# Attention with pooled keys and a squared-ReLU feed-forward: five blocks of chunk 0 in split form, eleven weight tiles used in place

## The chip, the cores and the metric

The kernel runs on one core of a Trainium2 chip. A core has five engines that run side by side, each with its own instruction queue, worked through in order: TensorE (PE: matrix products, and PEld for the loading of their weights), VectorE (DVE), ScalarE (ACT), GpSimd (POOL) and SyncE (SP, here a queue for DMAs only). They meet through semaphores. The metric is the device time of one execution, in microseconds.

## The reference

q, k and v have the shape (8 batches, 8 heads, 576 tokens, 64), all float32. Keys and values are averaged over 8 neighbouring tokens, so that 72 remain; attention goes over these, and the result feeds a network with 2048 hidden columns:

```python
k_p = k.reshape(B, H, Sp, pool, D).mean(axis=3)
v_p = v.reshape(B, H, Sp, pool, D).mean(axis=3)
scores = scale * np.matmul(q, k_p.transpose(0, 1, 3, 2))
scores = scores - np.max(scores, axis=-1, keepdims=True)
attn = np.exp(scores)
attn = attn / (np.sum(attn, axis=-1, keepdims=True) + 1e-09)
attn_out = np.matmul(attn, v_p)
...
x = np.ascontiguousarray(attn_out.transpose(0, 2, 1, 3)).reshape(B * S, H * D)
h = np.maximum(x @ w_in, 0.0)
return (h * h @ w_out).astype(np.float32)
```

x has 4608 rows and 512 columns. The weights arrive as eight-byte floats, taken as pairs of 32-bit words, and the kernel turns them into float32 itself.

## The kernel before

**Chunks, blocks and steps.** The 4608 rows are worked through in 9 chunks of 512 (`c`), the 2048 hidden columns in 16 blocks of 128 (`fc`). The main loop (lines 857 to 912) runs over 144 steps and three more, one step for each pair of chunk and block. In a step PE computes the first product of its block (`hidden`, tile h: x times w_in), then the attention work listed for that step (`on_pe`: scores, transposes of keys, the product with the values, av), then the second product of the block three steps back (`project`, tile o: the squared ReLU, r, times w_out; `LAG` is 3). Steps 0 to 15 are chunk 0, steps 16 to 31 chunk 1. The o of block 12 of chunk 0 is in step 15.

**Plain and split.** In chunk 0 both products take float32 operands as they are; the profile shows two records for each such matmul, 8 in a block's product. From chunk 1 on an operand is split into a rounded high part and the rest, both of type float32r, and three matmuls take the place of one: high times high, high times low, low times high (`three`, line 539), 12 in a block's product, in this order for each of four groups of 128 rows. The split of r makes gh (ACT copies) and gl (DVE subtracts); `split_hidden` (628) orders both two steps after the block's first product, gl through the list `behind`, which `catch_up` empties: in odd steps right after the second product, in even steps later. From chunk 2 on the first product is done with seven products in place of eight (`seven`), with sums that DVE and ACT make in PSUM (h, u).

**The weights.** A tile of w_out lands as raw words (`land`, SP queue), ACT takes two passes over it (`magnitude`), DVE three (`to_float32`: one TENSOR_SCALAR and two SCALAR_TENSOR_TENSOR). Several tiles of one step go through DVE together. The float32 tile wf_o serves chunk 0. Then `store_weights` (201) splits it into w_o (ACT copies, DVE subtracts), `send_weights` (206) writes w_o to DRAM (tile kept), and `fetch_weights` (211) brings it back for each later chunk, one step before its use. The steps of all this come from `need`: for tiles 11 to 15 of w_out the conversion is in steps 12, 13, 14, 15 and 16, `magnitude` one step before, `land` three before. `store_weights` of tile i is in step 10 + i, `send_weights` one later, and chunk 1 fetches tile i in step 18 + i.

**Buffers.** A pool of 40 slots in SBUF (`w_tile`) holds weights, raw tiles and operands. r has two buffers from chunk 1 on; in chunk 0 r uses the six of gh and gl. PSUM has eight banks: four for o, two for h, two of tag "a" for everything of the attention (keys kps, scores sps, turned exponents pps, av), which a tile holds until its last reader is through.

**Keys and scores.** `turn_k` (287) turns the pooled keys of a batch, pair of heads by pair, with a PE transpose into one bank (kps), and ACT copies them out (kf). For batch 1 this is `late_turn_k` (316) in step 3, at the end of the step, behind the second product. Pair 3 of these keys is the last that POOL sums up (kq). `token_scores` of chunk 1's pair 0 is in step 4 and takes both banks "a" (sps); DVE takes minima of them (tm), ACT eight exponents, four from each bank (te).

From chunk 2 on the stages of a pair of heads are `transpose_q` (DVE turns q into qs; ACT casts and DVE subtracts to get st), `scores` (PE; ACT copies sc out; POOL reduces it to the maximum, mx), `exponents` (DVE subtracts, ACT takes exponents, POOL reduces to the sum, tot), then the sums go through DRAM to a reciprocal that is broadcast (rs, rc, rr, rd, rb), and `weigh_values` (PE: av; DVE multiplies with rb into xf). `x_sums` and `x_operand` make of xf the operands x_B and x_T. `STEADY` and `EARLY` give the steps of the pairs, `START` holds back some of chunk 2.

**Order in a step.** `todo` holds what is due. Behind the second product and what follows from it come, in chunk 0, ReLU and square (`activate`), then loads, then the list in order of entry (`magnitude`, `send_weights`, `transpose_q`, `exponents`, ...), then `to_float32`, then the splits (`split_quarter` for w_in, `store_weights`); in chunk 1 `activate` follows behind these.

## Time and profile before

| | us |
|---|---|
| median of 3 runs | 910.28 (909.4 to 911.02) |
| profiled execution, time | 910.27 |
| profiled execution, span from first to last instruction | 908.5 |
| granted clock of PE, mean | 0.999 |
| PE / PEld / DVE / ACT / POOL busy | 894.3 / 715.2 / 568.1 / 509.6 / 421.1 |
| second product, plain (o<-wf_o,r), 128 records | 58.4 |
| second product, split (o<-w_o,gh and o<-w_o,gl), 1536 records | 322.3 + 200.9 |
| w_o<-kept, 128 transfers | 512 KB each |

The span is shared by PE's work and PE's gaps; all helpers record their instructions under one line (34), so the tables go by the names of tiles: `o<-w_o,gh` is the second product reading w_out's split tile and gh. In a timeline a row gives the start, the length, the engine, the operation, what it writes and reads, how many instructions are merged, and in square brackets the idle time before it with the engine and tile that ended it. Matmuls are pipelined, so a row's length overlaps the next one; the chain of waits gives the times from one to the next.

### The profile page before, as it was taken

To read this page: it belongs to the slowest core of one execution; us is meant where nothing else is said; L and a number is where in the kernel's file an instruction comes from. 1 tells how busy PE (TensorE), PEld (TensorE's weight loads), DVE (VectorE), ACT (ScalarE), POOL (GpSimd) and SP (SyncE) were. 2 spreads that over 40 slices of the span, in tenths; PEclk is the share of its full clock that TensorE was granted. 3 is DMA by queue.
4 is the path that set the end of the run, shared out by engine and by line. 5 is a ranking of instruction groups with operands and counts; after the bars stand their busy time and mean duration, and the time that the engine had idled before them with its cause. 6 is when DMAs were issued, how large, how long until landed. Compare 5 with 4: busy or idle time off the path is not lost.

```text
span 908.5 us, 14140 instructions
## 1 busy us (share of the span) xinstructions
PE 894.3 (98%) x5090; PEld 715.2 (79%) x5093; DVE 568.1 (63%) x946; ACT 509.6 (56%) x1017; POOL 421.1 (46%) x227
## 2 busy tenths in 40 slices
PE   8999999999999999999999999999999999999998
PEld 5444445777878888888888888888888888889987
DVE  7997778668688877456755575648544653353222
ACT  5866756656565656554655556455644564344442
POOL 3753245566555456566555655564444444200000
PEclk9999999999999999999999999999999999999999
DMA  9898574877555666665575556654533353245401
GB/s 222 263 261 189 140 177 110 229 227 196 130 155 141 143 143 142 178 156 118 133 207 135 120 143 179 153 132 117 170 109 113 105 164 116 96 173 197 175 1 47
DMA packets 157335, 138.72 MB, mean 153 GB/s; under 512 B 94488, under 2 KB 122136, under 8 KB 157264
## 3 DMA queue, kind: packets, MB, share of 16 engines
q1 hardware_dynamic: 128464, 127.13, 46.5%
q0 software_dynamic: 28800, 10.68, 10.3%
q8 instruction: 40, 0.66, 0.3%
q14 instruction: 31, 0.25, 0.1%
HBM read 119.65 MB, written 18.06 MB: 152 GB/s over the span
## 4 chain that ended last, share of the span: by engine, by line
PE 82%; DMA 6%; DVE 4%; ACT 2%; POOL 2%; issue 2%; SPq 1%; DVEq 0%; ACTq 0%; POOLq 0%
PE o L34 40%; PE h L34 35%; PE av L34 3%; PE sps L34 3%; SPq L34 1%; DMA rb<-rd 1%; POOL k L34 1%; DMA k<-in_k_dram 1%; DMA v<-in_v_dram 1%; DMA w_o<-kept 1%; DVE gl L34 1%; DVE wf_i L34 1%; DMA rd<-rr 1%; ACT sc L34 0%; DVE xf L34 0%
## 5 line engine op out<-in xcount | busy, mean ns | idle before, releaser
L34 PE MATMUL o<-w_o,gh 128*128 128x512 f32 x1024 | 322.3, 396 | 2.0 <-DMA w_o<-kept 2.0
L34 POOL PARTITION_ALL_REDUCE tot<-sc x56 | 187.8, 3403 | 86.4 <-issue 86.4
L34 PEld LDWEIGHTS o<-w_o,gh 128*128 128x128 f32 x1024 | 184.3, 188 | 46.8 <-issue 6.6
L34 PE MATMUL o<-w_o,gl 128*128 128x512 f32 x512 | 200.9, 392 | 0.0
L34 ACT ACTIVATE r<-h 128x512 f32<-128x512 f32 x144 | 83.6, 595 | 94.4 <-PE h L34 74.2
L34 PE MATMUL h<-x_T,w_S 128*128 128x256 f32 x1008 | 130.2, 283 | 0.5 <-ACT r L34 0.5
L34 POOL PARTITION_ALL_REDUCE mx<-sc x56 | 112.4, 2048 | 37.0 <-ACT sc L34 25.9
L34 PEld LDWEIGHTS h<-x_T,w_S 128*128 128x128 f32 x1008 | 124.9, 191 | 0.7 <-ACT r L34 0.7
L34 PEld LDWEIGHTS o<-w_o,gl 128*128 128x128 f32 x512 | 96.2, 188 | 21.3 <-DVE gl L34 0.4
L34 DVE TENSOR_TENSOR h<-h,u 128x256 f32<-128x256 f32 x168 | 72.6, 432 | 64.1 <-ACT u L34 33.7
L34 ACT COPY u<-h 128x256 f32<-128x256 f32 x112 | 41.8, 373 | 115.2 <-PE h L34 70.8
L34 PE MATMUL h<-x_B,w_A 128*128 128x256 f32 x672 | 98.6, 283 | 0.5 <-ACT r L34 0.5
L34 PEld LDWEIGHTS h<-x_B,w_A 128*128 128x128 f32 x672 | 91.6, 189 | 5.6 <-ACT r L34 1.1
L34 DVE TENSOR_TENSOR gl<-r,gh 128x512 fp32r<-128x512 f32 x128 | 92.1, 755 | 5.4 <-ACT gh L34 5.3
L34 POOL DMA_DIRECT2D k<-in_k_dram x36 | 44.1, 1225 | 109.1 <-issue 60.4
L34 POOL DMA_DIRECT2D v<-in_v_dram x36 | 44.1, 1224 | 107.4 <-issue 50.3
L34 DVE TENSOR_TENSOR u<-h,u 128x256 f32<-128x256 f32 x56 | 23.4, 417 | 101.9 <-ACT u L34 101.8
L34 ACT ACTIVATE r<-r 128x512 f32<-128x512 f32 x144 | 84.2, 625 | 1.1
L34 DVE TENSOR_TENSOR st<-qs,st 64x512 fp32r<-64x512 f32 x56 | 45.1, 806 | 61.8 <-ACT st L34 61.0
L34 ACT CAST gh<-r 128x512 fp32r<-128x512 f32 x128 | 78.9, 616 | 0.6 <-PE o L34 0.4
L34 ACT ACTIVATE sc<-sc 72x512 f32<-72x512 f32 x56 | 34.5, 632 | 69.3 <-DVE sc L34 69.3
L34 PE MATMUL h<-x,wf_i 128*128 128x512 f32 x128 | 57.8, 595 | 0.8 <-ACT x L34 0.8
(96 smaller groups left out, 1213.0 us busy)
## 6 DMA issues: line engine op xcount, KB each, us to landing
w_o<-kept SPq DMA_DIRECT2D x128, 512.0 KB
out_dram<-ob SPq DMA_DIRECT2D x36, 256.0 KB
raw_i<-in_moe_w_in_dram SPq DMA_DIRECT2D x16, 512.0 KB
raw_o<-in_moe_w_out_dram SPq DMA_DIRECT2D x16, 512.0 KB
kept<-w_o SPq DMA_DIRECT2D x16, 512.0 KB
rb<-rd SPq DMA_DIRECT2D x56, 128.0 KB
k<-in_k_dram POOLq DMA_DIRECT2D x36, 144.0 KB, 5.1
v<-in_v_dram POOLq DMA_DIRECT2D x36, 144.0 KB, 5.0
```

The costliest lines, as they stand in the source:

```text
L34: return lambda *a, **k: self.tc.keep_in_program_order(f(*a, **k))
```

## The change

Chunk 0's blocks from `WHOLE` = 11 on are treated as chunk 1's blocks are: r in its own two buffers, split into gh and gl, three matmuls in place of one. For that tiles 11 to 15 of w_out are converted in steps 12, 12, 13, 13 and 14, split in steps 12, 13, 13, 14 and 14 and written to DRAM in steps 13 to 17; chunk 1 fetches them as before. Tiles 0 to 10 are split in steps 16 to 26 instead of 10 to 20, written one step later, and chunk 1 reads the split tile where it is, without a fetch. Pair 3 of batch 1's keys is turned in step 4 instead of step 3, with a PSUM tile of its own. In chunk 1 `activate` comes ahead of the conversions and splits. For chunk 2, pair 0's `transpose_q` moves from step 9 to 8, pair 2's `transpose_q`, `scores` and `exponents` from 16, 18, 20 to 17, 19, 21; for chunk 3, pair 1's `exponents` and pair 2's `transpose_q` from step 32 to 33.

```diff
+    WHOLE = 11
...
-        stored[fc] = t
+        stored[fc] = wt["o", fc] = t
...
-    def late_turn_k(b):
-        turn_k(b)()
+    def late_turn_k(b, pairs=range(NPAIR)):
+        turn_k(b, pairs)()
...
-                if c == 0:
+                if c == 0 and f < WHOLE:
                     r = gts[c, f] = sb.tile([P, CH], F32, name=f"r_{c}_{f}", tag="gl" if f % 2 else "gh", bufs=3)
                 else:
                     r = gts[c, f] = sb.tile([P, CH], F32, name=f"r_{c}_{f}", tag="r", bufs=2)
...
     def split_hidden(c, fc):
-        if c == 0:
+        if c == 0 and fc < WHOLE:
             return
...
-            if c == 0:
+            if c == 0 and fc < WHOLE:
                 prods = [(g[:, tt], wf[key].rearrange("p a n -> p (a n)"))]
             else:
                 prods = [(g[x][:, tt], wt[key][:, w, :]) for x, w in three]
...
-    at(3, late_turn_k, 1)
+    at(3, late_turn_k, 1, range(NPAIR - 1))
+    at(4, late_turn_k, 1, [NPAIR - 1])
...
+    for i in range(WHOLE, NFC):
+        need["o", i] = WHOLE + 1 + (i - WHOLE) // 2
...
-        at(10 + i, store_weights, i)
-        at(11 + i, send_weights, i)
+        at(16 + i if i < WHOLE else (i + 14) // 2, store_weights, i)
+        at(17 + i if i < WHOLE else i + 2, send_weights, i)
...
-        for c in range(1, NCH):
+        for c in range(1 if i >= WHOLE else 2, NCH):
             at(c * NFC + i + LAG - STREAM, fetch_weights, c, i)
...
-    START = {transpose_q: 9, scores: 12, exponents: 13}
+    LATER = ((PLAIN + 1, 1, exponents), (PLAIN + 1, 2, transpose_q))
+    START = ({scores: 12, exponents: 13}, {}, {transpose_q: 17, scores: 19, exponents: 21}, {})
...
-                at(max(s + d, START[f]) if c == PLAIN and f in START else s + d - (f is transpose_q and (p != 2 if c >= PLAIN else p == 0)), f, c, p)
+                at(max(s + d, START[p].get(f, 0)) if c == PLAIN else s + d - (f is transpose_q and (p != 2 if c >= PLAIN else p == 0)) + ((c, p, f) in LATER), f, c, p)
...
+        if activate and s < PLAIN * NFC:
+            activate()
+            activate = None
```

## The prediction

> **What bounds the kernel now.** I read the page first, then PE's waits, then the chain that ended last, then each engine's timeline around the steps that the change touches. "Step s" is a turn of the main loop: the first product of block s, then the second product of block s − 3.

> ```profile
> PE 894.3 (98%) x5090; PEld 715.2 (79%) x5093; DVE 568.1 (63%) x946; ACT 509.6 (56%) x1017; POOL 421.1 (46%) x227
> DVE  7997778668688877456755575648544653353222
> ```

> PE is busy for 98% of the span. So a microsecond counts only if it is PE's own work or a gap of PE. DVE has room on average, but not in the first third (7 to 9 tenths), which is where the change puts more on it. The longest of PE's gaps, by what ended them:

> ```profile
> PE o L34 <- DMA w_o<-kept: 2.0, 2, 1.7
> PE sps L34 <- DVE xf L34: 1.5, 3, 0.9
> PE h L34 <- ACT r L34: 1.0, 2, 0.5
> ```

> With 0.8 us at kps (part 3) these 5.3 us hold every gap that the change can reach; beyond them only PE's own work can get less.

> **Part 1: five blocks of chunk 0 in split form.** From the chain of waits, with a plain second product (8 records), a split first product and a split second product (12 records):

> ```profile
> 143.92 3.43 PE o L34 x8
> 147.35 2.76 PE h L34 x12
> 150.12 3.43 PE o L34 x8
> ...
> 196.90 2.75 PE o L34 x12
> ```

> Plain costs 3.43 us a block, split 2.75, and next to each other they cost no more (143.92 to 150.12 is 3.43 + 2.76). Blocks 11 to 15: 5 × (3.43 − 2.75) = **−3.4 us**, PE's own work, so all of it on the path.

> **Part 2: the fetches of chunk 1.** Tiles 0 to 10 are now split at steps 16 to 26 and used in place, three steps later; 11 transfers of 512 KB are no longer issued.

> ```profile
> 191.16 0.71 PE L34 MATMUL o<-w_o,gh 128*128 128x512 f32 x2 [1.69 <-DMA w_o<-kept]
> 171.06 0.69 DVE L34 TENSOR_TENSOR w_o<-wf_o,w_o 128x512 fp32r<-128x512 f32 x1 [1.91 <-ACT w_o L34]
> 179.41 0.69 DVE L34 TENSOR_TENSOR gl<-r,gh 128x512 fp32r<-128x512 f32 x1 [0.38 <-ACT gh L34]
> ```

> The gap at 191.16 is step 22, tile 3. Its new split stands at step 19, where DVE does such a subtraction at 171, 20 us ahead, so **−1.7 us**. What is late next there is the gl of that block, and that is through at 180, 9 us before PE would ask for it. The 0.3 us that remain of the 2.0 belong to chunk 2 and stay. If the tile's place in DVE's order slipped by three steps, the gap would stay: 0 to −1.7.

> **Part 3: the last pair of batch 1's keys is turned one step later.** In step 3 PE waits for POOL's kq; in the new order pair 3 is turned at the end of step 4, behind the second product of block 1.

> ```profile
> 47.85 0.36 PE L34 MATMUL kps<-ident,kq 72*128 72x72 f32 x3
> 49.01 0.28 PE L34 MATMUL kps<-ident,kq 72*128 72x72 f32 x1 [0.80 <-POOL kq L34]
> 53.82 3.70 PE L34 MATMUL o<-wf_o,r 128*128 128x512 f32 x8
> 57.36 3.60 PE L34 MATMUL h<-x,wf_i 128*128 128x512 f32 x8
> ```

> The 0.8 goes. But the new kps needs a bank of tag "a", which has two, and in step 4 both hold the scores sps of chunk 1's pair 0. They come free when DVE has taken the minima and ACT the exponents:

> ```profile
> 58.07 0.81 DVE L34 TENSOR_REDUCE tm<-sps 128x4 f32<-128x288 f32 x2
> 58.60 1.80 ACT L34 ACTIVATE te<-sps,tm 128x72 f32<-128x72 f32 x8 [6.60 <-issue]
> ```

> The scores are through when PE's o starts, at 53.82, but DVE reaches the minima only at 58.07, and without a pause before them (the row has no idle time): it is still converting weights, and nothing ahead of them is changed. The first bank is free after four of eight exponents, 58.60 + 0.9 = 59.5, the second at 60.4. PE is there at 57.36 − 0.8 = 56.6, waits 2.9, turns the pair (about 0.25) and starts the next first product at 59.75 instead of 57.36: **+2.4 us** net. Behind the waiting kps stands all of PE. Bounds: −0.8 if no bank had to be waited for, +3.2 with the second bank. I take the first bank, the one that comes free first. PE's next gap is the one at 191.16, so this is not won back.

> **Part 4: DVE and ACT in steps 12 to 15.** Two tiles instead of one are converted in each of steps 12 and 13, and three more splits come ahead of the low half (gl) of block 12, which PE reads in step 15.

> ```profile
> 91.01 0.72 DVE L34 TENSOR_SCALAR wf_o<-wf_o 128x512 f32<-128x512 f32 x2
> 91.64 1.29 DVE L34 SCALAR_TENSOR_TENSOR wf_o<-wf_o,raw_o 128x512 uint32<-128x512 uint32 x2
> 92.85 1.28 DVE L34 SCALAR_TENSOR_TENSOR wf_o<-raw_o,wf_o 128x512 uint32<-128x512 uint32 x2
> ...
> 122.83 0.69 DVE L34 TENSOR_TENSOR x<-av,x 128x512 fp32r<-128x512 f32 x1 [3.30 <-ACT x L34]
> ...
> 132.47 3.77 DVE L34 SCALAR_TENSOR_TENSOR wf_o<-wf_o,raw_o 128x512 uint32<-128x512 uint32 x1
> 136.28 0.69 DVE L34 SCALAR_TENSOR_TENSOR wf_o<-raw_o,wf_o 128x512 uint32<-128x512 uint32 x1
> 136.88 2.73 DVE L34 TENSOR_TENSOR w_o<-wf_o,w_o 128x512 fp32r<-128x512 f32 x1
> 139.54 0.68 DVE L34 TENSOR_TENSOR w_A<-wf_i,w_A 128x512 fp32r<-128x512 f32 x1
> 140.14 1.25 DVE L34 TENSOR_TENSOR vp<-v 72x256 f32<-72x256 f32 x1
> 141.32 0.41 DVE L34 TENSOR_SCALAR wf_o<-wf_o 128x512 f32<-128x512 f32 x1
> 141.77 0.69 DVE L34 SCALAR_TENSOR_TENSOR wf_o<-wf_o,raw_o 128x512 uint32<-128x512 uint32 x1
> ```

> DVE's row of work starts when PE's av of step 12 is through (122.83, after a pause of 3.30), so it moves with PE and part 3 neither helps nor hurts it. gl of block 12 will come directly after the w_A whose successor starts at 140.14 now. New ahead of it: a pair of tiles (91.01 to 94.13, 3.1 us) for a single one (0.41 + 0.69 + 0.69 = 1.8), twice, +2.6; one more w_o and two gl at 0.6 each (139.54 to 140.14, start to start), +1.8. That gives 144.5.

> ```profile
> 123.87 0.66 ACT L34 ACTIVATE wf_o<-raw_o 128x512 f32<-128x512 f32 x1
> 124.42 0.67 ACT L34 ACTIVATE raw_o<-raw_o 128x512 uint32<-128x512 uint16 x1
> ```

> ACT has two more such passes over a raw tile (0.55 each from start to start) ahead of the casts of st, on which DVE then waits: half of their 1.1 reaches it, by my estimate, +0.6. POOL's next reduce, mx, now falls ahead of gl; beside it the vp at 140.14 took 1.25, of which I count 0.85 as lost, an estimate by the 0.41 that the next row needs for a tile of twice the size. Together about 146.0. PE reads gl as the third matmul of block 12: 143.92 − 0.68 (block 11 is shorter) + 0.46 = 143.7. So **+2.4 us**, rounded up by a semaphore's 0.1. Behind the waiting matmul stands all of PE; on ACT the r of block 13 waits for the gl of block 11 (two buffers r), behind it the exponents of chunk 2's pair 0 and POOL's sums, none of which PE reads before step 17. Afterwards steps 15 and 16 have no conversion any more (−1.8 each on DVE), and gl of block 13 comes out at about 151, when PE asks for it. Bounds: 0 if the sums move out of the way, and +5.9 from this:

> ```profile
> 133.04 7.02 POOL L34 PARTITION_ALL_REDUCE tot<-sc  x2
> 139.97 2.44 POOL L34 PARTITION_ALL_REDUCE mx<-sc  x1
> ```

> While POOL sums (7.02 us), three instructions of DVE of 0.69 take 3.77, 0.69 and 2.73: 5.1 us lost of the 7.02. Beside mx another of 0.69 (141.77) runs undisturbed. If each were held to the end of the reduces, DVE would lose 7.02 + 2.44 = 9.5 instead of 5.1 + 0.85 = 5.95, so 3.5 more, and PE would wait 5.9. [...]

> **Part 5: pair 2 of chunks 2 and 3 and pair 1's exponents a step later, relu and square ahead of the splits in chunk 1.** This touches two gaps at the start of chunk 2.

> ```profile
> 262.33 0.98 PE L34 MATMUL h<-x_B,w_A 128*128 128x256 f32 x6 [0.47 <-ACT r L34]
> 266.86 0.31 PE L34 MATMUL sps<-st,kl 128*72 128x192 f32 x1 [0.92 <-DVE xf L34]
> 270.15 0.88 PE L34 MATMUL h<-x_B,w_S 128*128 128x256 f32 x6
> 269.18 0.43 DVE L34 TENSOR_TENSOR h<-h,u 128x256 f32<-128x256 f32 x1 [0.44 <-ACT u L34]
> ```

> With the exponents and the transpose out of step 32, r and xf come sooner and both gaps (1.39) can close. But DVE's work from 253 to 270 is only reordered: its h at 269.6 is read by PE at 270.15, so only some 0.5 us can be won before this becomes the wait. **−0.5 us**; bounds −1.4 and +0.5 (st now stands closer to its scores, under POOL's sums).

> **Costed at nothing.** Five gl and gh of chunk 0 beyond block 12: DVE is ahead again. The raw tiles land up to two steps sooner: the SP queue has spare time there, since no store to DRAM waits in it before step 13. Pair 0's transpose for chunk 2 at step 8 instead of 9: a late q would hold DVE there, but the pause of 3.30 ahead of 122.83 takes up what DVE loses before it; without that pause it would be added to part 4.

> **Sum.** −3.4 − 1.7 + 2.4 + 2.4 − 0.5 = −0.8. The profiled execution took 910.27 (span 908.5 and 1.8 around it, which stays), the median is 910.28. Forecast: **909.5 us**, no change that counts; 0.2%, 1.8 us, is about what a measurement of this kernel can tell from none.

> **The rivals.**
> - DVE is in time for block 12 (its sums fall later, behind gl). For: ACT reaches the exponents about 3 us later than now. Against: even without ACT and mx gl comes at 144.5, unless less than the 5.1 us is lost ahead of it. Part 4 is 0: 907.1.
> - The turn of pair 3 meets a free bank. For: the old step 3 shows no wait for a bank. Against: two banks, two tiles of scores. Part 3 is −0.8: 906.3. With both, 903.9.
> - Slower: POOL's reduces hold DVE for their whole length in steps 13 and 14. Place: the third matmul of block 12; price 5.9 instead of 2.4; from 3.2 on the kernel is slower than before, from 5.0 on by more than 0.2%. 913.0. For: 3.77 and 2.73. Against: the 0.69 at 141.77.
> - The change doesn't do what it says: tile 3 is not ready in place and step 22 still waits. Against: 20 us of lead. 911.2.

> **How the numbers follow.** The forecast's case 0.55 (its own range 907.8 to 912.0 by the bank, part 5 and half a reduce more or less: 0.12 faster, 0.36 same, 0.07 slower); DVE in time 0.17; free bank 0.13; both 0.04; reduces that hold 0.08; no tile in place 0.03. Faster 0.46, same 0.39, slower 0.15. The range 905.5 to 912.3 leaves out the case of both, part of the reduces that hold and the ends of the rest.

> **What would show it.** Right: in PE's waits no w_o<-kept of 1.7; a kps that waits about 2.9 us for ACT te near 56.6; the o of block 12 waiting 2 to 3 us for DVE gl near 146; blocks 11 to 15 at 2.75 in the chain. Wrong: no wait at kps, no wait at gl, or PE gaps in chunk 1 at gl that the missing fetch had covered.

## The result and the profile after

| | before | after |
|---|---|---|
| median, 4 runs each | 910.19 (909.4 to 911.02) | 923.71 (920.92 to 924.89) |
| ratio, 95% interval | | 1.0144 (1.0119 to 1.0168) |
| profiled execution: time, span | 910.27, 908.5 | 923.6, 921.8 |
| PE busy | 894.3 | 897.7 |
| span less PE busy | 14.2 | 24.1 |
| granted clock of PE, mean | 0.999 | 0.994 |

The kernel is 13.3 us slower in span: 9.9 us of gaps, and 3.4 us more of PE's work, where the five split blocks should have made it 3.4 us less. First, PE's waits after the change, summed by what ended them (total, times, longest):

```profile
PE o L34 <- DVE gl L34: 5.8, 3, 3.1
PE kps L34 <- ACT te L34: 3.2, 1, 3.2
PE o L34 <- ACT ob L34: 1.8, 1, 1.8
PE h L34 <- ACT r L34: 1.5, 1, 1.5
PE o L34 <- DMA w_o<-kept: 0.9, 2, 0.7
```

The wait for the fetched tile (1.7) is gone, and so is the one for POOL's kq. The second is not the change's doing: of the 15 profiled executions here that turn all four pairs in step 3, seven have no such wait either, among them g3 and h3 below, which are the kernel before up to that step. The forecast's two new waits are there at 3.2 and 3.1. The other two waits for gl and the one for ob were not in the forecast. Where they are shows in PE's timeline after the change:

```profile
59.04 0.25 PE L34 MATMUL kps<-ident,kq 72*128 72x72 f32 x1 [3.19 <-ACT te L34]
59.13 5.34 PE L34 MATMUL h<-x,wf_i 128*128 128x512 f32 x8
150.36 0.50 PE L34 MATMUL o<-w_o,gl 128*128 128x512 f32 x1 [3.14 <-DVE gl L34]
152.76 2.88 PE L34 MATMUL h<-x,w_A 128*128 128x512 f32 x12
172.25 0.50 PE L34 MATMUL o<-w_o,gl 128*128 128x512 f32 x1 [2.13 <-DVE gl L34]
176.23 2.91 PE L34 MATMUL h<-x,w_A 128*128 128x512 f32 x12
181.86 0.73 PE L34 MATMUL o<-w_o,gh 128*128 128x512 f32 x2 [1.77 <-ACT ob L34]
```

The second row is the surprise. A first product in chunk 0 took 3.60 before; behind the wait at kps it takes 5.34. The table by stretches of time (PE, PEld, DVE, ACT and POOL busy with counts, then PE's granted clock, DMA share and GB/s) shows why:

```profile
60.00:64.00 4.00, 4.00 (x7) 1.54 (x5) 1.94 (x4) 2.76 (x6) 0.00 (x0) 0.58 1.11 347
150.30:153.00 2.70, 2.64 (x12) 2.19 (x13) 2.63 (x5) 2.26 (x4) 2.36 (x2) 1.00 0.49 178
172.20:175.60 3.40, 3.35 (x9) 2.63 (x10) 2.58 (x4) 2.07 (x4) 1.55 (x2) 0.56 0.51 125
181.80:185.20 3.40, 3.34 (x10) 2.67 (x11) 0.41 (x1) 3.37 (x8) 1.36 (x1) 0.65 0.76 282
```

The granted clock falls to 0.58, 0.56 and 0.65 for the stretch behind three of the four gaps; behind the one at 150 it stays at 1.00. In the chain that ended last two of these places show as slow products, beside a normal one of 12 records (start, length, records):

```profile
172.25 4.14 PE o L34 x10
...
181.86 4.60 PE o L34 x12
...
189.21 2.75 PE o L34 x12
```

The product at 172 had two of its 12 records ahead of the gap, so it has to be set against the ten records behind the gap at 150: from the gap's end to the next product they take 152.76 − 150.36 = 2.40 there and 176.23 − 172.25 = 3.98 here. So the three gaps cost 5.34 − 3.60 = 1.7, 3.98 − 2.40 = 1.6 and 4.60 − 2.75 = 1.9 on top of their own length. These 5.2 us are most of the 6.8 by which PE is busier than 894.3 − 3.4; the other 1.6 were not located.

From here on a **lead** is the start of a second product in the kernel before less that in the other kernel, both counted from their first second product (step 3), so that the start of an execution, which varies, drops out. It is worked out from PE's timelines, one profiled execution each. The execution of the kernel before has the wait of 0.8 for kq, so an execution that happens to lack it has a lead of 0.8 from step 4 on that no edit brought. For the changed kernel:

| step | 4 | 5 | 14 | 15 | 16 | 17 | 18 | 19 | 20 | 22 | 31 | 32 | end |
|---|---|---|---|---|---|---|---|---|---|---|---|---|---|
| lead, us | +1.1 | −4.1 | −4.1 | −3.0 | −6.1 | −7.2 | −5.6 | −11.8 | −13.5 | −11.6 | −11.7 | −12.8 | −13.7 |

Four places make it: the turn of the keys (between steps 4 and 5), gl of block 12 (15 to 16), the steps from 18 to 20, and a little at the entry of chunk 2. After step 22 nothing large happens.

The third place has a history of its own. VectorE after the change:

```profile
147.57 2.73 DVE L34 TENSOR_TENSOR gl<-r,gh 128x512 fp32r<-128x512 f32 x1
160.72 0.17 DVE L34 TENSOR_SCALAR rr<-rc 128x8 f32<-128x8 f32 x1 [3.78 <-DMA rc<-rs]
165.84 3.10 DVE L34 TENSOR_TENSOR w_o<-wf_o,w_o 128x512 fp32r<-128x512 f32 x1 [2.35 <-ACT w_o L34]
169.47 2.73 DVE L34 TENSOR_TENSOR gl<-r,gh 128x512 fp32r<-128x512 f32 x1
172.72 0.70 DVE L34 STREAM_TRANSPOSE qs<-q 128x512 f32<-128x512 f32 x1
```

gl of block 12 (147.57) is late, as forecast. But the softmax of chunk 2's pair 0 is late with it: its reciprocals (rr, 148.03 before) stand at 160.72, and DVE, in order, waits 3.78 for them. The next sum on POOL then covers w_o (3.10) and gl of block 15 (2.73, where such an operation alone takes 0.69), and PE has its gap at 172. ScalarE after the change carries it on:

```profile
173.45 1.26 ACT L34 CAST st<-qs 64x512 fp32r<-64x512 f32 x2 [6.60 <-DVE qs L34]
178.52 0.60 ACT L34 ACTIVATE r<-h 128x512 f32<-128x512 f32 x1 [0.98 <-DVE gl L34]
181.23 2.03 ACT L34 COPY ob<-o 128x512 f32<-128x512 f32 x4
```

ACT, in order, waits 6.60 for DVE's qs and then 0.98 for gl, and ob stands behind both. ob copies chunk 0's result out of the four banks o, which chunk 1's first second product overwrites. It stood at 167.95 before and stands at 181.23 now.

### The profile page after: what moved, and what is told of

It reads as the page before. It is cut to its first block, busy times and chain, and to the rows that moved or that the text cites. A ratio compares the mean times of both kernels' runs of the same rounds, so it can differ in the third digit from the quotient of the medians.

```text
span 921.8 us, 14170 instructions
## 1 busy us (share of the span) xinstructions
PE 897.7 (97%) x5110; PEld 721.1 (78%) x5113; DVE 574.4 (62%) x951; ACT 513.3 (56%) x1023; POOL 417.5 (45%) x227
## 4 chain that ended last, share of the span: by engine, by line
PE 68%; DVE 11%; DMA 8%; ACT 5%; issue 3%; SPq 3%; POOL 3%; DVEq 0%; ACTq 0%; POOLq 0%
PE o L34 33%; PE h L34 29%; PE av L34 3%; SPq L34 3%; DVE gl L34 2%; PE sps L34 2%; DMA w_o<-kept 2%; DMA v<-in_v_dram 2%; ACT r L34 1%; DMA k<-in_k_dram 1%; POOL k L34 1%; DVE xf L34 1%; DMA q<-in_q_dram 1%; DVE wf_i L34 1%; DVE st L34 1%
## 5 line engine op out<-in xcount | busy, mean ns | idle before, releaser
L34 PE MATMUL o<-w_o,gh 128*128 128x512 f32 x1064 | 337.9, 399 | 2.8 <-ACT ob L34 1.8
L34 PEld LDWEIGHTS o<-w_o,gh 128*128 128x128 f32 x1064 | 192.9, 189 | 50.8 <-issue 7.9
L34 POOL PARTITION_ALL_REDUCE tot<-sc x56 | 186.6, 3381 | 94.8 <-issue 94.8
L34 PE MATMUL o<-w_o,gl 128*128 128x512 f32 x532 | 210.4, 396 | 5.8 <-DVE gl L34 5.8
L34 ACT ACTIVATE r<-h 128x512 f32<-128x512 f32 x144 | 83.5, 594 | 101.9 <-PE h L34 67.9
L34 PE MATMUL h<-x_T,w_S 128*128 128x256 f32 x1008 | 130.5, 283 | 1.7 <-ACT r L34 1.5
L34 POOL PARTITION_ALL_REDUCE mx<-sc x56 | 111.0, 2027 | 42.0 <-ACT sc L34 33.9
L34 PEld LDWEIGHTS h<-x_T,w_S 128*128 128x128 f32 x1008 | 125.0, 191 | 2.1 <-ACT r L34 1.7
L34 PEld LDWEIGHTS o<-w_o,gl 128*128 128x128 f32 x532 | 100.8, 189 | 29.9 <-DVE gl L34 7.9
L34 DVE TENSOR_TENSOR h<-h,u 128x256 f32<-128x256 f32 x168 | 72.7, 433 | 63.0 <-ACT u L34 33.4
L34 ACT COPY u<-h 128x256 f32<-128x256 f32 x112 | 41.7, 372 | 117.6 <-PE h L34 70.6
L34 DVE TENSOR_TENSOR gl<-r,gh 128x512 fp32r<-128x512 f32 x133 | 100.7, 792 | 4.5 <-ACT gh L34 4.5
L34 PE MATMUL h<-x_B,w_A 128*128 128x256 f32 x672 | 98.5, 282 | 0.0
L34 PEld LDWEIGHTS h<-x_B,w_A 128*128 128x128 f32 x672 | 91.8, 189 | 4.8
L34 POOL DMA_DIRECT2D v<-in_v_dram x36 | 44.0, 1222 | 111.3 <-issue 48.8
L34 POOL DMA_DIRECT2D k<-in_k_dram x36 | 44.1, 1226 | 107.9 <-issue 49.6
L34 DVE TENSOR_TENSOR u<-h,u 128x256 f32<-128x256 f32 x56 | 23.4, 417 | 99.7 <-ACT u L34 99.5
L34 ACT ACTIVATE r<-r 128x512 f32<-128x512 f32 x144 | 84.3, 625 | 1.1
L34 DVE TENSOR_TENSOR st<-qs,st 64x512 fp32r<-64x512 f32 x56 | 46.4, 828 | 60.9 <-ACT st L34 60.0
L34 ACT CAST gh<-r 128x512 fp32r<-128x512 f32 x133 | 82.2, 618 | 0.6 <-PE o L34 0.4
L34 ACT ACTIVATE sc<-sc 72x512 f32<-72x512 f32 x56 | 34.5, 632 | 72.0 <-DVE sc L34 72.0
L34 PE MATMUL h<-x,wf_i 128*128 128x512 f32 x128 | 59.5, 610 | 0.8 <-ACT x L34 0.8
```

The lines of the kernel that those rows point to most:

```text
L34: return lambda *a, **k: self.tc.keep_in_program_order(f(*a, **k))
```

## The experiments

"Alone" below means one part of the change put into the kernel before, or one part undone in the changed kernel. Ratios are against runs of the kernel before on the same chip. The medians of two experiments can come from different chips (the kernel before lies between 909.48 and 911.26 on them), so where two experiments are compared the ratios go first.

### The turn of pair 3, and the clock

**e1_turn_back**: the changed kernel with all pairs turned in step 3.

```diff
-    at(3, late_turn_k, 1, range(NPAIR - 1))
-    at(4, late_turn_k, 1, [NPAIR - 1])
+    at(3, late_turn_k, 1)
```

> The changed kernel with all four pairs of batch 1's keys turned in step 3 again. Theory (three separate causes add up: the wait for a bank at the turn of pair 3, DVE's lateness from block 12 on, and PE's clock after a gap): the wait of 3.2 us and some 1.7 us of slow matmuls behind it go, 0.8 us at kq comes back, so about 4.1 us less than the changed kernel, 919.6. Rival (DVE, ACT and POOL alone set the pace of chunk 0, PE would only wait longer at gl): no more than 1 us less, and the waits at gl grow by what is won.

920.50, ratio 1.0117 (1.0088 to 1.0146). The wait at kps and the slow product behind it are gone. The forecast was 4.1 us less; it is 2.5 by the ratios (whose intervals overlap), 3.2 by the medians, 5.6 by the two profiled executions (918.02 against 923.6). Most of the loss stays, and the wait for ob is even longer, 4.72 instead of 1.77: it has a cause of its own.

**e2_awake**: the changed kernel with twelve matmuls of PE that nobody reads (`still`, into the bank that the next first product overwrites) between the second product of step 4 and the late turn.

```diff
+    def fill_gap(n):
+        t = early[0, 5] = ps_h.tile([P, 512], F32, name="h_0_5", tag="h")
+        keep_awake(0, t, n)
...
+    at(4, fill_gap, 12)
```

> The changed kernel with 12 matmuls on zeros (bf16, 512 columns, some 0.22 us each) into the bank of the next first product, ahead of the late turn of pair 3, so that PE is not idle while it waits there. Theory (a gap of some 2 us lowers the granted clock for the next 3.4 us): the first product behind the turn takes 3.6 us again instead of 5.3, granted clock 1.00 there, and the kernel loses about 1.7 us, 922.0. Rival (the slow product comes from its operands or from traffic, not from the gap): it stays at 5.3 us and the time at 923.7 or above.

922.31, ratio 1.0141 (1.0110 to 1.0172), which can't be told from the changed kernel by its time. The profile shows more. PE's timeline of e2_awake, and then the stretch that showed 0.58 above:

```profile
60.31 0.23 PE L34 MATMUL kps<-ident,kq 72*128 72x72 f32 x1
60.38 3.65 PE L34 MATMUL h<-x,wf_i 128*128 128x512 f32 x8
```

```profile
60.00:64.00 4.00, 4.00 (x16) 1.55 (x13) 3.61 (x7) 2.27 (x8) 0.00 (x0) 1.00 1.01 235
```

The first product behind the wait takes 3.65 instead of 5.34 and the clock stays at 1.00. The lead in step 5 is −1.6 instead of −4.1: 1.7 us of that are the clock, and 0.8 come from a bank that is free sooner here (14.4 us after the first second product instead of 15.2). This one trace doesn't show that the added matmuls kept the clock up: g4 below has the same late turn without them, waits 2.42 at kps, and its first product also takes 3.65 at a clock of 1.00. What the two traces differ in is in the last section; by the estimate there, they were needed here. The wait for ob is 4.6 here, as in e1.

### How many blocks are split

**e3_whole16** splits none of chunk 0's blocks (`WHOLE = 16`), **e4_whole14** two (`WHOLE = 14`, their tiles split one step later); both with the turn in step 3.

```diff
-    WHOLE = 11
+    WHOLE = 16
```

> The changed kernel with the turn in step 3 and with WHOLE = 16: no block of chunk 0 in split form, all 16 tiles of w_out split in steps 16 to 31 and used in place by chunk 1. Theory (the loss comes from the split blocks' work on DVE and ACT in steps 12 to 15 and from the turn): chunk 0 is as before, the wait of 1.7 us for w_o is gone, 907.5 to 909. Rival (the loss comes from the other moves: stores, ReLU ahead of the splits, pair 2 and the exponents a step later): 914 or more.

> The changed kernel with the turn in step 3 and with WHOLE = 14: only blocks 14 and 15 of chunk 0 in split form, tiles 14 and 15 converted and split in step 15. Theory (DVE's load ahead of the first gl decides, and two blocks put less of it there): 1.4 us less than with WHOLE = 16 if gl comes in time, 906.5; up to 909 with a wait of some 2 us at gl of block 14. Rival (any split block in chunk 0 brings the lateness with its knock-on waits): 912 or more.

917.24, ratio 1.0075 (1.0047 to 1.0103), and 916.01, ratio 1.0076 (1.0035 to 1.0117). Both theories miss, and both rivals have the time right (914 or more, 912 or more). In e3 nothing is lost up to the end of chunk 1 (lead +0.8 in step 31), then 7 us go between steps 31 and 32. So a kernel with no split block and the turn undone is still slower. But e3 is not simply the rest of the change: it also splits tiles 11 to 15 in steps 27 to 31, right ahead of the place where it loses (e4 does so with tiles 11 to 13 and loses 6 there; e1, which doesn't, loses 0.9). How much of the change's own loss lies outside the blocks, e3 can't tell. PE's timeline of e3_whole16 there:

```profile
251.18 0.38 PE L34 MATMUL h<-x_T,w_S 128*128 128x256 f32 x1 [1.56 <-ACT x_T L34]
255.00 2.93 PE L34 MATMUL h<-x_T,w_S 128*128 128x256 f32 x12 [2.24 <-ACT r L34]
```

PE waits for ACT, in the steps that lead into chunk 2; the row of 2.93 takes 1.69 in the kernel before.

### Conversions, pair 2, and the fetches

**f2_convert_sooner**: e1 with tiles 11 to 15 converted one step sooner. **f1_pair2_back**: e1 with pair 2 of chunk 2 at its old steps. **f3_both**: both.

```diff
-        need["o", i] = WHOLE + 1 + (i - WHOLE) // 2
+        need["o", i] = WHOLE + (i - WHOLE) // 2
...
-    START = ({scores: 12, exponents: 13}, {}, {transpose_q: 17, scores: 19, exponents: 21}, {})
+    START = ({scores: 12, exponents: 13}, {}, {}, {})
```

> e1_turn_back with tiles 11 to 15 of w_out landed and converted one step sooner (11, 11, 12, 12, 13), splits as they are, so that the first pair falls into DVE's pause of 4.5 us in step 11 to 12. Theory (DVE's lateness at gl of block 12 begins all that follows): the wait of 2.7 us at gl falls under 0.5, the later waits shrink with it, 5 us or more less than e1, at most 915.5. Rival (the waits at the entry to chunk 1 have a cause of their own): only the 2.7 us go, 918, and the wait for ob stays near 4.7.

> e1_turn_back with chunk 2's pair 2 at its old steps again (transpose_q 16, scores 18, exponents 20). Theory (the wait of 4.7 us for ACT's copies ob at chunk 1's first o comes from the transpose in step 17, whose st DVE has to finish under POOL's sums ahead of the gl on which ACT's r waits): that wait falls under 1.5 us and the slow clock behind it goes, 4 to 6 us less than e1, 914.5 to 916.5. Rival (the lateness that began at gl of block 12 is handed on by DVE and ACT whatever stands in step 17): the wait stays at 4 us or more, 920.

> f1 and f2 together. Theory (both are needed: the load on DVE in steps 12 to 14 and the transpose in step 17): no wait over 0.7 us at gl or ob before chunk 2; five blocks in split form then give their 3.4 us and the missing fetch 1.7, less 1 to 2 us at the entry to chunk 2: 906 to 907.5. Rival (one of them suffices): the better of f1 and f2, within 1 us.

f2: 916.01, ratio 1.0048 (1.0028 to 1.0067). f1: 919.63, 1.0084 (1.0056 to 1.0113). f3: 914.67, 1.0039 (1.0018 to 1.0060). Converting sooner brings 6.3 us against e1 by the ratios (4.5 by the medians, 920.50 to 916.01) and ends the wait for gl of block 12 for the most part (1.2 left in f2, none in f3). Pair 2 brings 3.0 by the ratios and 0.9 by the medians (f1 against e1), 0.8 and 1.3 (f3 against f2), with intervals that overlap both times, and its theory fell: with it back, ob still waits 4.1 in f3, and in f1 a wait of 3.55 of the scores for xf stands where ob's was. Something else holds ACT.

**f4_in_place**: the kernel before with part 2 alone (tiles 0 to 10 split in steps 16 to 26, used in place in chunk 1).

```diff
-        at(10 + i, store_weights, i)
-        at(11 + i, send_weights, i)
+        at(16 + i if i < 11 else 10 + i, store_weights, i)
+        at(17 + i if i < 11 else 11 + i, send_weights, i)
...
-        for c in range(1, NCH):
+        for c in range(1 if i >= 11 else 2, NCH):
```

> The kernel before with part 2 alone: tiles 0 to 10 split in steps 16 to 26 and used in place by chunk 1, tiles 11 to 15 stored and fetched as before, nothing else. Theory (part 2 takes away the wait of 1.7 us and adds nothing): 1.5 us less than before at the start of chunk 2 and at the end. Rival (the splits that end in step 26 instead of 25 and double in steps 21 to 25 make ACT's r late at the start of chunk 2): the 1.7 us are given back there, same as before.

911.26, ratio 0.9999 (0.9979 to 1.0020): no change. The forecast's 1.7 is there, 1.84 us of lead between steps 21 and 22, but 1.3 are lost between steps 9 and 11 and most of the rest goes in waits under 1 us in chunks 1 to 5.

### What holds ScalarE

Two theories were left. V: with the stores of tiles 0 to 4 gone from steps 11 to 15, SP runs ahead and loads queries into the time in which POOL adds up v. R: `activate` ahead of the splits in chunk 1 makes ACT wait for gl with everything else behind it.

**g1_q_behind**: f3 with the queries of pair 2 behind the first store. **g3_before_q_sooner**: the kernel before with these queries in step 10. **g4_after_q**: the changed kernel with them in step 14.

```diff
-            at(s - 2 if c < PLAIN else max(s - QL, 8), load_q, c, p)
+            at(s - 2 if c < PLAIN else 13 if (c, p) == (PLAIN, 2) else max(s - QL, 8), load_q, c, p)
```

(10 and 14 in the other two; in g1 tile 11 is also split and stored one step sooner.) **g2_relu_behind**: f3 without these lines:

```diff
-        if activate and s < PLAIN * NFC:
-            activate()
-            activate = None
```

> The kernel of f3_both (914.67; turn of batch 1 undivided, conversions a step sooner, pair 2 of chunk 2 at its old steps), with the queries of chunk 2's pair 2 loaded in step 13 instead of 12, and tile 11 split in step 11 and stored in step 12, so that this store stands ahead of those queries on SP as the store of tile 0 did in the kernel before. Theory V: with the stores of tiles 0 to 4 gone from steps 11 to 15 SP no longer waits there, its loads of queries go out at 102 instead of 116 us and share the DMA engines with the sums of v on POOL (v from 110 instead of 104, mx from 131.8 instead of 124.3, tot from 140.5 instead of 133.0); all of ACT's and DVE's late work in steps 13 to 18 follows from that. Then here v's second load is near 105, mx starts near 125 to 127 and tot near 134 to 136, the wait of 4.1 for ACT ob at the first second product of chunk 1 is under 1.5, and the time is 908 to 911. Rival R: ob is late because relu stands ahead of the splits in chunk 1 and ACT waits there for gl; then mx may be sooner but the wait for ob stays at 3 to 5 and the time at 913.5 to 915.5.

> The kernel of f3_both with relu and square of chunk 1 again behind the splits, as in the kernel before; nothing else. Rival R: the wait for ACT ob (4.1) is gone or under 1 and so is the wait of 2.2 for ACT r at chunk 2's entry; 907 to 910. Theory V: mx still starts near 131.8, ob still waits 2.5 or more; only the entry of chunk 2, where ACT waits for gl ahead of the x operands, can get better, by up to 3; 911 to 915.

> The kernel before with one edit: the queries of chunk 2's pair 2 loaded in step 10 instead of 12, so that they stand ahead of the first stores on SP. Theory V: they go out near 101 to 104 us instead of 116, the first load of v that POOL adds starts some 3 us later or more, mx starts at 128 to 132 instead of 124.3 and tot near 137 to 140; PE, which in this kernel has no split block before chunk 1, loses 0 to 3, 910 to 913. Rival: the loads of queries take nothing from v, mx stays within 1 us of 124.3 and the time within 1 us of the kernel before.

> The changed kernel (923.7) with one edit: the queries of chunk 2's pair 2 loaded in step 14 instead of 12, behind the first store that is left (tile 11). Theory V: mx, at 131.9 there with PE 4.1 late, starts near 127 to 129, gl of block 12 is read without a wait over 1.5, the waits for gl of 3.1 and 2.1 and for ob of 1.8 with their slow clocks are gone or halved; 914 to 919. Rival: the delay comes from the raw tiles that land sooner, or from DVE's own added work; then mx stays near 131 and the time over 921.

| | us | ratio (95%) | mx of pair 0 starts at | ob waits |
|---|---|---|---|---|
| f3_both, for comparison | 914.67 | 1.0039 (1.0018 to 1.0060) | 131.8 | 4.1 |
| g1_q_behind | 916.43 | 1.0060 (1.0039 to 1.0081) | 128.9 | 3.1 |
| g2_relu_behind | 910.67 | 1.0005 (0.9987 to 1.0024) | 131.7 | none |
| g3_before_q_sooner | 912.09 | 1.0018 (0.9993 to 1.0042) | 128.3 | none |
| g4_after_q | 924.53 | 1.0154 (1.0113 to 1.0195) | 129.7 | 1.9 |

V has its first step right and its price wrong. The queries do delay POOL (in g3, where nothing else is changed, mx comes at 128.3 instead of 124.34), but the time does not follow: g1 and g4 are no faster than the kernels that they mend, and g3 can't be told from the kernel before. R holds: with `activate` back, the wait for ob is gone although mx is as late as ever. ScalarE and VectorE in f3_both, at the place of the wait:

```profile
168.42 0.60 ACT L34 ACTIVATE r<-h 128x512 f32<-128x512 f32 x1 [3.86 <-DVE gl L34]
171.13 2.03 ACT L34 COPY ob<-o 128x512 f32<-128x512 f32 x4
```

```profile
162.59 2.55 DVE L34 TENSOR_TENSOR w_o<-wf_o,w_o 128x512 fp32r<-128x512 f32 x1 [1.30 <-ACT w_o L34]
165.06 0.68 DVE L34 TENSOR_TENSOR w_A<-wf_i,w_A 128x512 fp32r<-128x512 f32 x1
165.66 2.72 DVE L34 TENSOR_TENSOR gl<-r,gh 128x512 fp32r<-128x512 f32 x1
170.22 0.69 DVE L34 TENSOR_TENSOR w_o<-wf_o,w_o 128x512 fp32r<-128x512 f32 x1 [1.83 <-ACT w_o L34]
```

And in g2_relu_behind:

```profile
166.13 0.60 ACT L34 ACTIVATE r<-h 128x512 f32<-128x512 f32 x1 [1.30 <-DVE gl L34]
167.81 2.04 ACT L34 COPY ob<-o 128x512 f32<-128x512 f32 x4
```

```profile
161.96 3.53 DVE L34 TENSOR_TENSOR w_A<-wf_i,w_A 128x512 fp32r<-128x512 f32 x1
165.41 0.68 DVE L34 TENSOR_TENSOR gl<-r,gh 128x512 fp32r<-128x512 f32 x1
166.01 2.73 DVE L34 TENSOR_TENSOR w_o<-wf_o,w_o 128x512 fp32r<-128x512 f32 x1
```

The relu of a block takes one of two buffers r, so it has to wait until DVE has made gl from that buffer, two blocks earlier. With relu first, the casts of w_o and w_A stand behind it on ACT. ACT waits 3.86 for DVE's gl, and then DVE waits 1.83 for ACT's w_o: each is idle for the other. With the casts first, DVE has its next operands while POOL's sum holds it, and works through (no wait in its three rows). ob comes 3.3 us sooner, and PE finds it done. By the ratios g2 is 3.1 us faster than f3.

### Relu alone, and the entry of chunk 2

**h2_after_relu**: the changed kernel without the three lines. **h3_before_relu_ahead**: the kernel before with them. **h1_relu_and_q**: g1 and g2 together. **h4_no_later**: h1 with

```diff
-    LATER = ((PLAIN + 1, 1, exponents), (PLAIN + 1, 2, transpose_q))
+    LATER = ()
```

**h5_mended** is h1 again, in more runs.

> The changed kernel (923.7) with relu and square of chunk 1 behind the splits again; nothing else. Theory: the edit costs here what it cost in f3_both, 4 or more, since the blocks are later still: the waits for gl of 2.1 and for ob of 1.8 in steps 18 and 19 go with the slow clock behind them; 917 to 920. Rival: these waits come from the late sums of the softmax on SP and DVE, which stay; 921 to 924.

> The kernel before with one edit: relu and square of chunk 1 ahead of the splits. Theory: ACT waits there for gl at each step in which DVE is under a reduce, ob is late at the first second product of chunk 1 and the entry of chunk 2 is late; 2 to 5 slower, 912 to 915. Rival: the edit costs only where DVE and POOL are already late by the change; then within 1.5 of the kernel before.

> The kernel of g2_relu_behind (910.67; profiled 3.4 us lost between the second products of steps 31 and 32) with the queries of chunk 2's pair 2 behind tile 11's store, as in g1_q_behind. Theory: POOL, whose reduces ran 7 us later from step 13 on, stays late through chunk 1, and its sums meet DVE's low halves at the entry of chunk 2; with the queries behind the store the loss there is 1 or less instead of 3.4: PE 4.0 ahead of the kernel before at the end of chunk 1 and 2.5 to 4 ahead at the end; 906.5 to 908.5. Rival: the loss at the entry is a matter of the steps of chunks 2 and 3 alone; then it stays at 3 or more and the time at 910 to 911.

> The kernel of h1_relu_and_q with pair 1's exponents and pair 2's transpose of chunk 3 at their old steps. Theory: they stand in step 32, behind the entry's loss, and change at most the gaps of 0.5 to 0.9 in steps 33 and 34: within 1 of h1_relu_and_q. Rival: they cause the loss at the entry; then h1 is at 910 to 911 and this one 2 or more below it.

> The kernel of h1_relu_and_q once more, with more rounds. If the 3.6 us of its profiled execution are its rule: ratio 0.995 to 0.998, interval below 1. If the lead over the kernel before is given back at the entry of chunk 2 in most executions, as in g2_relu_behind and h4_no_later: ratio 0.998 to 1.001, and in this profile PE loses 3 or more between the second products of steps 31 and 32.

| | us | ratio (95%) | lead in step 22 | 31 | 32 | end |
|---|---|---|---|---|---|---|
| h2_after_relu | 919.46 | 1.0091 (1.0072 to 1.0110) | −5.7 | −5.6 | −5.6 | −7.5 |
| h3_before_relu_ahead | 913.73 | 1.0039 (1.0018 to 1.0061) | +2.5 | +1.1 | −2.2 | −2.1 |
| g2_relu_behind | 910.67 | 1.0005 (0.9987 to 1.0024) | +4.1 | +4.0 | +0.6 | +1.0 |
| h1_relu_and_q | 911.46 | 0.9985 (0.9965 to 1.0005) | +4.0 | +4.0 | +4.0 | +3.6 |
| h4_no_later | 909.65 | 0.9986 (0.9966 to 1.0006) | +5.9 | +5.6 | +1.1 | +1.0 |
| h5_mended | 909.68 | 0.9996 (0.9974 to 1.0019) | +4.9 | +5.2 | +1.5 | +1.7 |

Relu alone costs 0.39% of the kernel before (3.6 us), and taken out of the changed kernel it gives back 0.53%, 4.8 us (923.71 − 919.46 = 4.3 by the medians). h3's interval leaves out 1, and those of h2 and the changed kernel don't meet. In h3 the loss is not at ob but at the entry of chunk 2, where ACT's relu waits 4.37 for gl (1.35 before) and the x operands stand behind it. ScalarE in the kernel before and in h3:

```profile
242.63 0.60 ACT L34 ACTIVATE r<-h 128x512 f32<-128x512 f32 x1 [1.35 <-DVE gl L34]
```

```profile
245.11 0.60 ACT L34 ACTIVATE r<-h 128x512 f32<-128x512 f32 x1 [4.37 <-DVE gl L34]
```

mx of pair 0 starts at 124.32 in h3, as in the kernel before (124.34): a late POOL in chunk 0 is not needed for this loss.

h1's profile alone would say that its two edits mend the entry. They don't: h5 is the same kernel, and its profiled execution loses 3.7 us there. Of five profiled executions with relu behind (g2, h1, h2, h4, h5) three lose 3.4 to 4.5 and two, h1 and h2, nothing; neither theory of the entry is borne out, since h1 and h5 differ in nothing. DVE's rows show what differs between h1_relu_and_q, where nothing is lost, and h4_no_later, in that order:

```profile
236.00 0.69 DVE L34 TENSOR_TENSOR wf_i<-wf_i 128x512 f32<-128x512 f32 x1
236.60 0.69 DVE L34 TENSOR_TENSOR w_S<-wf_i,w_S 128x512 fp32r<-128x512 f32 x1
```

```profile
236.80 1.53 DVE L34 TENSOR_TENSOR wf_i<-wf_i 128x512 f32<-128x512 f32 x1
238.25 0.68 DVE L34 TENSOR_TENSOR w_S<-wf_i,w_S 128x512 fp32r<-128x512 f32 x1
```

POOL's mx starts at 236.97 in the one and 236.70 in the other. In h1 DVE is through with wf_i ahead of it, in h4 it is caught. ACT's relu then comes at 238.77 or at 240.41, PE waits 0.58 or 2.24 for the next one, and behind 2.24 its product takes 2.93 instead of 1.70. In f3_both the same product also takes 2.93 behind a wait of 2.24, and the granted clock there was 0.50. The difference begins one sum earlier, and it separates all five: where nothing is lost (h1, h2), POOL's sum tot holds DVE at a w_S (3.62 and 3.63) and mx starts 2.7 us behind that sum; in g2, h4 and h5 it holds the gl behind that w_S (3.21, 3.65 and 3.62), and mx starts 1.6 behind it. This is argued from five profiles; no run moved that meeting by itself.

## Why the prediction was wrong

909.5 was forecast, in a range of 905.5 to 912.3; 923.71 was measured. None of the rivals had the time either.

**Part 1 holds.** Between steps 14 and 19 the lead grows by 3.4 in h4_no_later, as worked out, by 2.2 to 2.4 in g2 and h5, and by 1.4 in h1, where a wait of 1.6 for ob takes most of the rest.

**Part 2 holds** (1.84 or 1.85 against 1.7) in every kernel here that has it. But the fetched tile is not late in every execution: h3, which keeps the fetches, gains 1.7 at the same place. What part 2 freed for SP, which the forecast costed at nothing, moves POOL: mx starts at 133.3 in f4 (part 2 alone, in an execution whose first second product is 2.3 later) and at 128.3 in g3, instead of 124.3, without a price in time that these runs can tell.

**Part 3: mechanism and wait hold, the price does not.** The bank came free at 59.0 where 59.5 was forecast, the wait is 3.19 against 2.9 (2.4 in h2 and g4, with the same turn). The step that failed is that a gap was priced at its length. The granted clock behind it fell to 0.58 and took 1.7 more: −4.1 in place of −2.4. The same term is missing at two of the later gaps, 5.2 us in all. It doesn't come in every execution (it does in h2, not in g4, by the same turn). The 0.8 at kq that the sum took off was not there to be won: it comes and goes without the change.

**Part 4: right at gl of block 12, wrong behind it.** 3.14 against 2.4, and PE read gl at 150.4 with PE already 3.0 late, where 146.0 was forecast from a PE in time. The 0.1 counted for a semaphore was 0.06 there (gl ends at 150.30, PE starts at 150.36). The step that failed is the line under what was costed at nothing: "Five gl and gh of chunk 0 beyond block 12: DVE is ahead again." The softmax stages late behind it made DVE wait 3.78 at rr and put POOL's next sum over gl of block 15. Conversions a step sooner (f2 against e1) give back 6.3 by the ratios, 4.5 by the medians.

**Part 5 is the step whose failure is shown best**, since h3 has it alone. It weighed relu and square ahead of the splits only at two gaps of chunk 2, by DVE's work, and came to −0.5 with bounds of −1.4 and +0.5. It never asked what on ACT stands behind a relu that has to wait for its buffer. h2, h3 and f3 against g2 give 4.8, 3.6 and 3.1 us by the ratios, on the other side. Of the exponents and the transpose set a step later nothing could be seen (h1, h4, h5).

**The slower rival** (reduces that hold DVE, 913.0) named the right contact, POOL's sums over DVE's subtracts, at one place; it recurs at blocks 12 and 15. DVE is still not held throughout: during the sum over block 12, two reduces from 143.85 to 150.74, a w_A at 146.97 takes its 0.68.

One after the other, the edits that were taken back bring the ratio from 1.0144 to 1.0117 (turn), 1.0048 (conversions), 1.0039 (pair 2) and 1.0005 (relu). That is nearly all of the loss, and still not the gain: with a lead of 4 to 6 us at the end of chunk 1, g2, h4 and h5 lose 3.4 to 4.5 at the entry of chunk 2, and no version was found that is faster than the kernel before beyond its interval. Of these steps only the conversions are clear of the intervals by themselves; h2 and h3 show the relu's share. Open are what decides that entry from execution to execution, and 1.6 us of PE's busy time in the changed kernel.

## What to carry to other kernels

A gap of PE cost its length and, behind three of the four shown of the changed kernel, a slow stretch on top, 1.6 to 1.9 us; where a gap can't be avoided, matmuls that nobody reads can fill it (behind them the first product took 3.65 in e2 instead of 5.34), though e2's time alone shows no gain. An instruction that is moved ahead on an engine with one queue takes its waits along (relu on ACT in f3_both: 3.86, with ob behind it): price what stands behind it when the wait is long, not its own time. A lead won in one stage is kept only if the engines that feed the next stage have won it too.

## What the runs showed of the hardware

```profile
171.50:175.20 3.70, 3.44 (x9) 2.72 (x10) 1.79 (x3) 3.67 (x8) 2.18 (x2) 0.54 0.72 254
253.60:256.60 3.00, 2.92 (x13) 2.92 (x14) 1.21 (x4) 2.97 (x7) 0.49 (x1) 0.50 0.43 49
```

It did not fall behind 3.14 at 150 in the changed kernel, nor behind the 1.69 at 191 in the kernel before (1.00 in both stretches). So in these runs the length of a gap alone did not decide. The plainest pair is h2_after_relu, which waits 2.43 at kps and loses the clock, and g4_after_q, which waits 2.42 there and keeps it. In that order:

```profile
56.16:59.57 3.41, 0.98 (x4) 0.18 (x3) 3.41 (x8) 1.79 (x8) 1.45 (x1) 1.00 0.60 87
59.57:62.98 3.41, 3.41 (x5) 1.34 (x5) 2.76 (x6) 1.84 (x6) 0.00 (x0) 0.50 1.12 259
```

```profile
54.56:57.97 3.41, 2.22 (x6) 0.67 (x4) 3.41 (x6) 0.00 (x0) 2.15 (x3) 1.00 0.78 186
57.97:61.38 3.41, 2.18 (x6) 1.12 (x7) 3.41 (x8) 3.21 (x12) 0.00 (x0) 1.00 1.07 325
```

In these traces the slow stretches begin and end on a grid. In the changed kernel the clock falls to 0.50 or rises to 1.00 at 59.97, 63.38, 172.61, 176.02, 182.85 and 186.26: on a grid of 3.413 us these are 0, 1, 33, 34, 36 and 37 steps from the first. In all nine traces here with more than one slow stretch (e1, e2, e4, f1, f2, f3, g4 and h2 beside it) every change lies on such a grid to 0.02 us, and where the grid lies differs from execution to execution. The 15 traces with a slow stretch, cut on their grids from 44 to 430 us, give 1649 windows at full clock. Behind 28 of them the clock is halved, and in each of these PE was busy for 0.48 of the window or less; in all the others it was busy for 0.48 or more. So in these traces a gap cost the clock when it left PE idle for about half of one window: h2's gap falls into one (0.98 of 3.41 busy), g4's is shared by two (2.22 and 2.18). In the changed kernel PE was busy for 0.93, 1.28 and 1.64 of the 3.41 ahead of the three slow stretches, and for 1.92 and 1.77 in the two windows of the gap at 150, where the clock stayed at 1.00. The bound is no sharper than such figures. In e2 the window from 57.82 to 61.23 holds the wait, with PE's work from 60.31 on and almost none before; without the added matmuls it would be about 0.3 busy, an estimate from these rows, and by the 28 windows above the next one would be slow.
